# Second scores of a pack-attention soft-MoE kernel in eight small tiles, with wider rows of p, two more weight chunks on chip, plain 32-row output products and products of ones in waits

## The chip, the core and the metric

The kernel runs on one core of a Trainium2 chip. The core has TensorE (PE, matrix products, with its weight loads PEld), VectorE (DVE), ScalarE (ACT), GpSimd (POOL) and SyncE (SP, which here only issues transfers). The metric is the device time of one execution in microseconds (us). All data are float32. A float32 product stands in the trace as two instructions, a transpose as one.

## The reference

Eight batches of eight heads, 576 positions, head dimension 64, 32 packing queries p; then 32 slots on 8 experts.

```python
def sm_attn(qq, kk, vv):
    s = scale * np.matmul(qq, kk.transpose(0, 1, 3, 2))
    s = s - np.max(s, axis=-1, keepdims=True)
    a = np.exp(s)
    a = a / (np.sum(a, axis=-1, keepdims=True) + 1e-09)
    return np.matmul(a, vv)
p_packed = sm_attn(p, k, v)
out = sm_attn(q, p_packed, p_packed)      # second scores: q against p_packed
# x: [4608, 512], phi: [512, 32]
logits = x @ phi
d = softmax(logits, axis=0); slot_input = d.T @ x
for e in range(E):                        # 8 experts, 4 slots each
    slot_out[e] = np.maximum(slot_input[e] @ w1[e], 0.0) @ w2[e]
c = softmax(logits, axis=1)
return c @ slot_out
```

## The kernel before

**Attention in eight steps.** Step i takes two batches and four heads (dd = i // 2 is the pair of batches, g = i % 2 the group of heads). Each step consists of small functions, and the text ORDER lists their calls as name.i.j@bank:engine; each engine works through its own instructions in that order. The functions that the text names: `kt` transposes k on DVE, `s1` are the first scores, `mx1` and `e1` maximum and exponential, `ap`/`apc` transpose the result and copy it, `m` multiplies with v, `ppa`/`pp`/`pt`/`ptc` give the normalized packed values and their transpose ppT, `mp`/`mm` multiply ppT with phi, `qp`/`qc` transpose and copy q, `s2` (L548) are the second scores, `sc` copies them out, `st` (L573) transposes them back, `mx2`, `sb` (L608), `e2` (L631), `z2`, `rc` (L649, L650) and `n2` (L654) make the second softmax, `a2p` (L663) and `a2c` its transpose.

**Logits and slots, once for each pair of batches.** `lg` (L687) adds up the logits of a pair, `f1` to `f6` and `fd` the running softmax over positions, `gr` (L788), `rt`, `gt` (L810), `rb`, `gs` (L847) and `sa` the slot inputs, from which the last call makes xz.

**Experts.** `layer1a` (L934) multiplies xz with w1, `hidden` and `layer1b` transpose and rectify, `layer2` (L986) multiplies with w2 into one bank; `cq`/`cp` (L1004 to L1012) transpose the weights c of the 36 row blocks, split into a high and a low part. The last expert goes to banks of its own in two halves (L1077), is copied (L1095) and summed over its four strips by products with rep (L1098), the sum is split into a high and a low part (L1100, L1101), and 36 output products (L1122, L1129) are copied to the ring and stored.

**Transfers.** SP issues all loads in a fixed list: p of pair 0, k of step 0, the three other p, q and v of step 0, then k, q, v of each step, then w1 and w2 in chunks of 1 MB (32 in all, the last as two halves). They go to a ring of 14 chunks; a load is issued when the space next in the ring is free, which the last reader of a k, q, v or weight piece reports. At the call `late` six further chunks go to `ext`, in the space that the attention's tiles leave. At most eight transfers are under way: each waits for the one eight before it. phi is loaded on ACT's queue at the start.

A second score of step i, for the part j of the row blocks (4, 1 and 4 of the nine), is in before four products over all 128 rows into 64 columns, of which half of the 128 rows are zeros in ppT:

```python
nc.tensor.matmul(
    ps[64 * x : 64 * x + 64, bank, c : c + R * (n1 - n0)].rearrange("p (n r) -> p n r", n=n1 - n0),
    ppTs[i % 2][:, x, b2, o : o + 2].rearrange("p v s -> p (v s)"),
    qT[:, b2, n0:n1, 64 * x : 64 * x + 64], start=True, stop=True)
```

Of the kernel before, what the change touches and what calls it, by code (L numbers as in the profile page):

```python
# [100 lines left out]
def pack_attention_soft_moe(  # L101
# [1067 lines left out]
```

## Time and profile before

| what | value |
|---|---|
| median of three runs | 213.82 us (213.2 to 216.62) |
| the profiled execution, its own time | 215.42 us |
| its span, first to last instruction | 213.6 us |
| mean granted TensorE clock | 0.927 |
| busy: PE, DVE, ACT, POOL | 175.1, 129.8, 102.8, 47.7 us |
| moved by the DMA engines | 72.27 MB, 338 GB/s over the span |

The page cuts the span in 40 slices of 5.34 us; a digit is a busy share in tenths, PEclk the granted TensorE clock in tenths of full speed (9 is 90% or more, 5 the lower of its two levels, 1.2 of 2.4 GHz). A busy PE is not PE at its peak, since matrix products are pipelined and their ends modelled. The attention runs to about 130 us, the last logits and slots to 147.65 us, the experts to 184.85 us, the output from 187.81 us on.

### The profile page before, as it was taken

To read this page: it belongs to the slowest core of one execution; us is meant where nothing else is said; L and a number is where in the kernel's file an instruction comes from. 1 tells how busy PE (TensorE), PEld (TensorE's weight loads), DVE (VectorE), ACT (ScalarE), POOL (GpSimd) and SP (SyncE) were. 2 spreads that over 40 slices of the span, in tenths; PEclk is the share of its full clock that TensorE was granted. 3 is DMA by queue.
4 is the path that set the end of the run, shared out by engine and by line. 5 is a ranking of instruction groups with operands and counts; after the bars stand their busy time and mean duration, and the time that the engine had idled before them with its cause. 6 is when DMAs were issued, how large, how long until landed. Compare 5 with 4: busy or idle time off the path is not lost.

```text
span 213.6 us, 5804 instructions
## 1 busy us (share of the span) xinstructions
PE 175.1 (82%) x2403; PEld 114.8 (54%) x2403; DVE 129.8 (61%) x306; ACT 102.8 (48%) x250; POOL 47.7 (22%) x75
## 2 busy tenths in 40 slices
PE   2399899999799999999999975776999999797000
PEld 1177586877656966768887555343233433374000
DVE  1649578979468786986547698245722475299000
ACT  3035656969539758859656564120211111289000
POOL 7200002754006363063171554003000000000000
PEclk9999999999999999999999997558799999999655
DMA  6999999999999999978429999950699999169997
GB/s 168 283 375 394 391 391 389 388 391 387 394 388 390 391 394 408 347 264 315 183 88 413 361 414 420 426 242 0 218 423 428 422 419 407 47 230 410 410 421 299
DMA packets 24730, 72.27 MB, mean 338 GB/s; under 512 B 4224, under 2 KB 4480, under 8 KB 22784
## 3 DMA queue, kind: packets, MB, share of 16 engines
q1 hardware_dynamic: 24128, 71.83, 87.5%
q8 instruction: 19, 0.31, 0.6%
q10 hardware_dynamic: 576, 0.07, 0.2%
q14 instruction: 7, 0.06, 0.1%
HBM read 62.46 MB, written 9.44 MB: 337 GB/s over the span
## 4 chain that ended last, share of the span: by engine, by line
PE 44%; DMA 25%; DVE 14%; ACT 7%; issue 2%; ACTq 0%; SPq 0%; DVEq 0%
DMA ring<-in_moe_w_dram 13%; PE ps L524 6%; DMA ring<-in_k_dram 6%; PE ps L433 6%; PE ps L663 4%; PE ps L548 3%; PE ps L1129 3%; DMA phi_sb<-in_moe_phi_dram 3%; PE ps L380 3%; DMA ring<-in_v_dram 3%; PE ps L573 3%; PE ps L788 3%; PE ps L934 3%; DVE kT L366 2%; PE ps L411 2%; PE ps L687 2%
## 5 line engine op out<-in xcount | busy, mean ns | idle before, releaser
L366 DVE STREAM_TRANSPOSE kT<-ring 128x576 f32<-128x576 f32 x32 | 23.0, 754 | 6.7 <-DMA ring<-in_k_dram 5.2
L331 ACT COPY qT<-ps 128x512 f32<-128x512 f32 (+1 forms) x45 | 20.6, 492 | 10.9 <-PE ps L524 10.6
L639 POOL TENSOR_TENSOR zt<-a 128x576 f32<-128x576 f32 x7 | 10.0, 1426 | 69.6 <-ACT a L631 51.0
L524 PE MATMUL ps<-ident,ring 128*128 128x128 f32 x144 | 22.9, 292 | 0.7 <-DVE a L608 0.5
L548 PE MATMUL ps<-qT,ppT 128*64 128x256 f32 (+1 forms) x192 | 19.0, 335 | 1.2 <-ACT ppT L331 1.0
L524 PEld LDWEIGHTS ps<-ident,ring 128*128 128x128 f32 x144 | 17.5, 151 | 4.1 <-issue 2.1
L433 PE MATMUL ps<-ring,a1T 64*64 64x128 f32 x576 | 18.3, 273 | 1.6 <-DVE a L608 1.3
L654 POOL TENSOR_TENSOR a<-a,zs 128x1152 f32<-128x1152 f32 (+1 forms) x8 | 16.4, 2050 | 11.2 <-DVE zs L650 7.4
L380 PE MATMUL ps<-kT,pT 32*32 32x288 f32 x512 | 14.9, 446 | 4.2 <-DVE kT L366 4.2
L433 PEld LDWEIGHTS ps<-ring,a1T 64*64 64x64 f32 x576 | 15.6, 133 | 4.1 <-DVE a L608 1.5
L580 DVE TENSOR_REDUCE mx<-ps 128x16 f32<-128x512 f32 (+1 forms) x24 | 12.9, 543 | 3.8 <-PE ps L573 3.4
L548 PEld LDWEIGHTS ps<-qT,ppT 128*64 128x64 f32 x192 | 11.0, 136 | 7.6 <-issue 3.3
L934 PE MATMUL ps<-ring,xz 128*32 128x512 f32 x112 | 14.2, 660 | 0.6 <-DVE xz L1019 0.6
L331 ACT COPY a1T<-ps 128x384 f32<-128x384 f32 x24 | 10.9, 487 | 5.9 <-PE ps L411 5.8
L331 ACT COPY a2T<-ps 128x384 f32<-128x384 f32 x24 | 10.7, 491 | 6.0 <-PE ps L663 5.9
L663 PE MATMUL ps<-ident,a 128*128 128x128 f32 x72 | 11.4, 296 | 2.2 <-DVE a L654 2.2
L391 DVE TENSOR_REDUCE nm<-ps 128x2 f32<-128x1152 f32 x8 | 10.7, 1344 | 3.3 <-PE ps L380 3.3
L331 ACT COPY s2T<-ps 128x512 f32<-128x512 f32 (+1 forms) x19 | 9.2, 491 | 6.3 <-PE ps L548 6.3
L608 DVE TENSOR_TENSOR a<-ps,mx 128x256 f32<-128x256 f32 x32 | 11.9, 418 | 0.4
L380 PEld LDWEIGHTS ps<-kT,pT 32*32 32x32 f32 x512 | 7.0, 107 | 9.3 <-issue 4.8
L394 ACT ACTIVATE a<-ps,nm 128x576 f32<-128x576 f32 x16 | 11.8, 746 | 0.3 <-DVE nm L391 0.3
L573 PE MATMUL ps<-ident,s2T 128*128 128x128 f32 x72 | 11.7, 278 | 0.2
(143 smaller groups left out, 296.4 us busy)
## 6 DMA issues: line engine op xcount, KB each, us to landing
ring<-in_moe_w_dram SPq DMA_DIRECT2D x25, 1024.0 KB, 8.5
ring<-in_k_dram SPq DMA_DIRECT2D x16, 576.0 KB, 11.9
ring<-in_q_dram SPq DMA_DIRECT2D x16, 576.0 KB, 11.9
ring<-in_v_dram SPq DMA_DIRECT2D x16, 576.0 KB, 12.0
out_dram<-ring SPq DMA_DIRECT2D x10, 768.0 KB, 8.5
ext<-in_moe_w_dram SPq DMA_DIRECT2D x6, 1024.0 KB, 13.8
ring<-in_moe_w_dram SPq DMA_DIRECT2D x2, 512.0 KB, 17.9
out_dram<-ring SPq DMA_DIRECT2D x2, 512.0 KB, 4.7
```

The lines of the kernel that those rows point to most:

```text
L331: nc.scalar.copy(dst, src)
L366: nc.vector.transpose(kT[:, b2, :, c].rearrange("p m (t r) -> p m t r", t=T), view(f"k{i}.{b2}").rearrange("p (m t c d) -> p m t c d", m=2 ...
L380: nc.tensor.matmul(ps[32 * y : 32 * y + 32, z, 0 : 32 * T], pT[rs, dd, m, b2, g, c], kT[rs, b2, m, c], start=(c == 0), stop=(c == 1),)
L433: nc.tensor.matmul(ps[64 * b2 : 64 * b2 + 64, b + x, 0:P].rearrange("p (m d) -> p m d", m=2), a1T[rs, t, b2], view(f"v{i}.{b2}").rearrange ...
L524: nc.tensor.transpose(ps[:, bank, o : o + P], view(f"q{i}.{b2}")[:, P * n : P * n + P], ident)
L548: nc.tensor.matmul(ps[64 * x : 64 * x + 64, bank, c : c + R * (n1 - n0)].rearrange("p (n r) -> p n r", n=n1 - n0), ppTs[i % 2][:, x, b2, o ...
L573: nc.tensor.transpose(ps[:, bank, o : o + P], s2T[:, n].rearrange("p b r -> p (b r)"), ident)
L580: nc.vector.tensor_reduce(mxs[i % 2][:, n0:n1].rearrange("p n a -> p (n a)"), ps[:, banks["st", i, j], 0 : P * (n1 - n0)].rearrange("p (a ...
L608: nc.vector.tensor_tensor(a[:, x, j // 2 : T - 1 + j // 2, 1 - j // 2].rearrange("p (n v) s -> p n v s", v=2), src[:, x], m[:, x].unsqueez ...
L654: (nc.vector if eng == "v" else nc.gpsimd).tensor_tensor(a, a, z.unsqueeze(3).broadcast_to([P, a.shape[1], a.shape[2], NS]), op=ALU.mult)
L663: nc.tensor.transpose(ps[:, bank, o : o + P], a2s[i // NG % 2][:, t, i % NG].rearrange("p c s -> p (c s)"), ident,)
L934: nc.tensor.matmul(ps[32 * a : 32 * a + 32, b + nh, :], xzf[:, (4 * e + a) * NSLOT : (4 * e + a + 1) * NSLOT], wv[:, j, nh * 512 : (nh + 1 ...
```

## The change

1. `s2` for the parts 0 and 2 is called per batch b2 instead of per part and gives both: 8 products of 64 rows into 32 columns, in two row groups that write two banks, so 16 in place of 8 a step; the zero half of ppT is no longer multiplied. Part 1 stays at four products over 128 rows. `s1` is called in two halves (by batch), `lg` in two (by step), `gt` makes eight products of half width, `px` works in 32-row groups and once for the pairs 1 to 3.
2. p is loaded as 128 rows of 1024 bytes (before 512 pieces of 256 bytes). phi's four loads move from ACT's queue to SP's, behind v of step 0.
3. `late` gives seven chunks to `ext`; one more chunk (the second of w1 of expert 3) goes to the tile a2_1 at the call `lx`, behind the last `gr`. xz, hidden and the slot sums move into tiles of the attention.
4. `w` calls stand in the waits at the start and in the last logits: products of ones, w.n of 128 n columns, whose results nobody reads.
5. c is transposed as plain float32, four row blocks in one (9 transposes in place of 36), the high and low parts go, the last expert adds to the bank of the others, and each output product takes 32 rows: four of them stand in four row groups.
6. ORDER is written anew. The last `n2` of step 7 is on DVE in both of its parts (before one was on POOL).

```diff
     def f_s2(i, j, bank, eng):
-        for b2 in range(2):
-            for x in range(2):
...
-                    ppTs[i % 2][:, x, b2, o : o + 2].rearrange("p v s -> p (v s)"),
-                    qT[:, b2, n0:n1, 64 * x : 64 * x + 64],
+        b2 = j // 2
+        for x in range(2):
+            for m in range(2):
+                n0, n1 = nk(2 * m)
+                for u in range(2):
+                    us = slice(64 * u, 64 * u + 64)
+                    a = 2 * x + (u + m) % 2
+                    nc.tensor.matmul(
+                        ps[
+                            32 * a : 32 * a + 32,
+                            banks["s2", i, 2 * u],
+                            4 * R * b2 : 4 * R * b2 + 4 * R,
+                        ].rearrange("p (n r) -> p n r", n=4),
+                        ppTs[i % 2][us, x, b2, 2 * (1 - m) + u],
+                        qT[us, b2, n0:n1, 64 * x : 64 * x + 64],
...
     def rows_p(dd):
-        return p[2 * dd : 2 * dd + 2].rearrange("b (g h) s d -> (h s) (b g) d", g=NG)
+        return p[2 * dd : 2 * dd + 2].rearrange("b h (s j) d -> (b h s) (j d)", j=4)
...
+    def f_lx(i, j, bank, eng):
+        key = f"w1_{LX[0]}_{LX[1]}"
+        where[key] = (a2f, 2 * FF)
+        load(a2f[:, 0 : 2 * FF], rows_w1(*LX))
...
-    for x, xs in enumerate(halves):
-        nc.scalar.copy(sh[:, xs], ps[:, 2 + x, xs])
-        nc.vector.tensor_tensor(sh[64:P, xs], ps[64:P, 2 + x, xs], shf[64:P, xs], op=ALU.subtract)
+    for x, (xs, eng) in enumerate(zip(halves, "va")):
+        copy(eng, sh[:, xs], ps[:, 2 + x, xs])
...
-            nc.tensor.matmul(ps[:, b], cT[:, dd * T + order[t]], sh, start=True, stop=True)
+                nc.tensor.matmul(ps[:, b], cT[rs, n4], sh[rs], start=True, stop=True)
```

Two lines of ORDER, the last ones after the change:

```
a2p.7.2@5 rb.2.0 a2c.7.2:a w.1.0@0 gs.2.0 lg.3.1 xz.0.0 sa.2.0
f1.3.0 w.2.0@0 f2.3.0 f3.3.0 w.4.0@0 w.1.0@0 f4.3.0 f5.3.0
```

**Where instructions stand on PE, step 1.** First before, from the packed values of step 1 (L475) on: L548 is s2, with columns and elements of the output behind the names.

```order
L475 MATMUL ps<-ident,pp_157 128x128 x2
L380 MATMUL ps<-kT,pT 32x288 x32
L548 MATMUL ps<-qT,ppT_161 64x256 x8
L548 MATMUL ps<-qT,ppT_161 64x64 x4
L497 MATMUL ps<-phi_sb,ppT_161 64x32 x4
L573 MATMUL ps<-ident,s2T 128x128 x4
```

And in the changed kernel, where L505 is pt, L595 and L578 are s2's two forms and L410 is s1 (of the next steps):

```order
L505 MATMUL ps<-ident,pp_158 128x128 x2
L527 MATMUL ps<-phi_sb,ppT_162 64x32 x4
L595 MATMUL ps<-qT,ppT_162 32x256 x16
L554 MATMUL ps<-ident,ring 128x128 x4
L410 MATMUL ps<-kT,pT 32x288 x16
L622 MATMUL ps<-ident,s2T 128x128 x4
```

Eight products into 64 columns have become sixteen into 32, and part 1 (L578) stands some rows further down, apart from them.

**Where instructions stand on PE, last logits and slots.** Before, from the transposes of the last second softmax (L663) to the first product with w1 (L934):

```order
L663 MATMUL ps<-ident,a_1_109 128x128 x9
L847 MATMUL ps<-rb,pp_156 64x64 x2
L847 MATMUL ps<-rb,pp_157 64x64 x2
L687 MATMUL ps<-a2T_153,mm_162 32x288 x4
L687 MATMUL ps<-a2T_154,mm_163 32x288 x4
L699 MATMUL ps<-ident,nml 1x128
L721 MATMUL ps<-ones,m_185 128x1
L729 MATMUL ps<-dm,ones 128x32
L760 MATMUL ps<-rw,ones 128x32
L788 MATMUL ps<-a_1_109,d 32x256 x18
L810 MATMUL ps<-rep,rt 128x32 x4
```

After it, from the first half of lg (L732) on; L866 are the products of ones:

```order
L732 MATMUL ps<-a2Tb,mm_163 32x288 x4
L866 MATMUL ps<-ones 128x384
L708 MATMUL ps<-ident,a_1_117 128x128 x6
L866 MATMUL ps<-ones 128x128
L708 MATMUL ps<-ident,a_1_117 128x128 x3
L866 MATMUL ps<-ones 128x128
L893 MATMUL ps<-rb,pp_157 64x64 x2
L893 MATMUL ps<-rb,pp_158 64x64 x2
L732 MATMUL ps<-a2Tb,mm_164 32x288 x4
L866 MATMUL ps<-ones 128x256
L744 MATMUL ps<-ident,nml 1x128
L866 MATMUL ps<-ones 128x512
```

The first half of lg has moved ahead of the last transposes, of which only three stand behind the last n2, and products of ones stand between all of these.

**SP's queue at the start**, after the change (L182 is phi, L173 all other loads):

```order
L173 DMA ring<-in_p_dram 128x256
L173 DMA ring<-in_k_dram 128x2x576 x2
L173 DMA ring<-in_p_dram 128x256 x3
L173 DMA ring<-in_q_dram 128x2x576 x2
L173 DMA ring<-in_v_dram 128x2x576 x2
L182 DMA phi_sb<-in_moe_phi_dram 64x2x32 x4
```

phi's four issues are new in this queue, behind v of step 0 and ahead of k of step 1; the p issues stand where they stood.

## Rows read from the trace of the kernel before

**Rows 1.** The page, part 2: granted clock and GB/s in 40 slices of 5.34 us.
```profile
PEclk9999999999999999999999997558799999999655
GB/s 168 283 375 394 391 391 389 388 391 387 394 388 390 391 394 408 347 264 315 183 88 413 361 414 420 426 242 0 218 423 428 422 419 407 47 230 410 410 421 299
```
**Rows 2.** Windows by stage: length, busy us (instructions) by engine, granted clock, DMA share, GB/s.
```profile
28.00:122.00 94.00, 91.23 (x1575) 69.31 (x1575) 70.42 (x171) 66.68 (x168) 34.41 (x38) 1.00 0.93 348
98.00:112.00 14.00, 13.85 (x263) 11.88 (x261) 7.53 (x24) 9.63 (x26) 5.45 (x7) 1.00 0.45 165
132.20:147.65 15.45, 11.12 (x92) 6.67 (x92) 5.78 (x21) 2.98 (x9) 2.07 (x2) 0.58 0.65 268
147.65:184.85 37.20, 36.64 (x328) 13.76 (x328) 18.70 (x44) 5.27 (x8) 0.00 (x0) 0.95 0.83 339
184.85:187.81 2.96, 1.90 (x7) 1.25 (x8) 1.28 (x3) 1.49 (x4) 0.00 (x0) 1.00 0.00 0
187.81:213.60 25.79, 8.50 (x36) 5.92 (x34) 9.49 (x16) 9.89 (x20) 0.00 (x0) 0.73 0.91 367
```
**Rows 3.** Timeline of the issuing queues (SPq, ACTq): start us, us, what.
```profile
1.04 1.38 ACTq L273 DMA_DIRECT2D phi_sb<-in_moe_phi_dram  x2
2.28 4.71 SPq L169 DMA_DIRECT2D ring<-in_p_dram  x3
109.35 0.88 SPq L169 DMA_DIRECT2D ring<-in_moe_w_dram  x2
120.99 8.09 SPq L169 DMA_DIRECT2D ext<-in_moe_w_dram  x6
150.57 16.59 SPq L169 DMA_DIRECT2D ring<-in_moe_w_dram  x13
```
**Rows 4.** DMA queues, ACT's own (phi): packets, MB, share of 16 engines' span.
```profile
q10 hardware_dynamic: 576, 0.07, 0.2%
```
**Rows 5.** The chain that ended last: start us, us, what.
```profile
15.36 12.56 DMA ring<-in_k_dram
...
60.21 0.38 PE ps L548 x8
...
114.52 1.01 PE ps L548 x8
...
117.83 1.25 PE ps L548 x16
```
**Rows 6.** Groups by line on PE: rows*columns of the array, count, busy us, mean ns.
```profile
L433 PE MATMUL ps<-ring,a1T 64*64 64x128 f32 x576 | 18.3, 273 | 1.6 <-DVE a L608 1.3 <-ACT a1T L331 0.3
L548 PE MATMUL ps<-qT,ppT 128*64 128x256 f32 x128 | 16.4, 388 | 1.2 <-ACT ppT L331 1.0 <-DVE a L600 0.2
L380 PE MATMUL ps<-kT,pT 32*32 32x288 f32 x512 | 14.9, 446 | 4.2 <-DVE kT L366 4.2
L1012 PE MATMUL ps<-identr,c 128*128 128x128 f32 x36 | 4.6, 257 | 0.2
```
**Rows 7.** Timeline of the last logits and slots: start us, us, instruction, count.
```profile
120.67 1.18 PE L687 MATMUL ps<-a2T,mm 128*32 128x288 f32 x16
126.60 1.49 PE L788 MATMUL ps<-a,d 64*32 64x256 f32 x36
129.98 1.21 DVE L649 TENSOR_SCALAR zs<-zs 128x12 f32<-128x12 f32 x1
131.49 0.56 DVE L654 TENSOR_TENSOR a<-a,zs 128x384 f32<-128x384 f32 x1
132.19 2.15 PE L663 MATMUL ps<-ident,a 128*128 128x128 f32 x9 [2.16 <-DVE a L654]
134.90 2.15 PE L687 MATMUL ps<-a2T,mm 128*32 128x288 f32 x16
141.70 2.77 PE L788 MATMUL ps<-a,d 64*32 64x256 f32 x36
```
**Rows 8.** Timeline of the end: the subtraction that makes the low part.
```profile
186.51 0.86 DVE L1101 TENSOR_TENSOR sh<-ps,sh 64x256 fp32r<-64x256 f32 x2 [1.20 <-ACT sh L1100]
```

More of the change, by code (lines that the diff above doesn't have):

```diff
@@ L176, in pump @@
             key, width, src = loads[state["next"]]
+            if key == "phi":
+                nc.sync.dma_start(out=width, in_=src)
+                state["next"] += 1
+                continue
             if "at" not in state:
@@ new lines, in layer2 @@
+    def layer2(e, js=range(NJ)):
+        last = e == E - 1
+        for xs in halves if last else (slice(0, DM),):
+            for j in js:
+                a = (j + 2 * (xs.start > 0)) % 4
+                nc.tensor.matmul(
+                    ps[32 * a : 32 * a + 32, SO, xs],
+                    hTf[:, (NJ * e + j) * NSLOT : (NJ * e + j + 1) * NSLOT],
+                    w2v(e, j)[:, xs],
+                    start=(e == 0 and j < 4),
+                    stop=(last and j >= 6),
+                )
+        for j in js:
+            if j % 4 == 3 and not last:
+                release(f"w2_{e}_{j // 4}")
@@ L1019, in pack_attention_soft_moe, with cp @@
+    def cp(n0, n1, eng):
+        bank = 6 + n0 // 4 % 2
+        for n in range(n0, n1):
+            nc.tensor.transpose(
+                ps[:, bank, (n - n0) * P : (n - n0 + 1) * P],
+                Lf[:, 4 * n : 4 * n + 4].rearrange("p t s -> p (t s)"),
+                ident,
+            )
+        copy(
+            eng,
+            cT[:, n0:n1].rearrange("p n x -> p (n x)"),
+            ps[:, bank, 0 : (n1 - n0) * P],
+        )
     nc.vector.tensor_tensor(
@@ L1047, in pack_attention_soft_moe @@
     layer2(1)
+    layer2(2)
     ees.close()
@@ L1102, in pack_attention_soft_moe @@
+    for xs, eng in zip(halves, "va"):
+        copy(eng, so[:, xs], ps[:, SO, xs])
+    for x, xs in enumerate(halves):
+        nc.tensor.matmul(ps[:, 2 + x, xs], repf, so[:, xs], start=True, stop=True)
+    for x, (xs, eng) in enumerate(zip(halves, "va")):
+        copy(eng, sh[:, xs], ps[:, 2 + x, xs])
     for key in ("w2_7_0", "w2_7_2", "w2_7_3"):
         release(key)
-    obank = [4, 5, 6, 7, 0, 1, 2, 3]
-    load = {"a": 0.0, "v": 0.0}
-    order = [4 * (t % 2) + t // 2 for t in range(T - 1)] + [T - 1]
+    obank = [4, 6, 7, 0, 1, 5, 2, 3]
@@ L1109, in pack_attention_soft_moe @@
+    work = {"a": 0.0, "v": 0.0}
     n = 0
```

491 lines of the change are left out of this document (230 added, 261 removed).

## The prediction

> **What bounds the kernel now.** I read the windows by stage first, then the GB/s slices, the queue of SP, the chain, and last the groups by line.
>
> From 28 to 122 us PE is busy for 91.23 of 94 us, DVE for 70.4 and ACT for 66.7 [rows 2]. This stage, steps 2 to 7 of the attention, is PE's. Ahead of it the loads set the pace: the chain holds k of step 2 from 15.36 to 27.92 us [rows 5], and the first two slices of the GB/s row stand at 168 and 283 against some 391 later [rows 1]. Later the loads run ahead until the ring is full: from 98 to 112 us only 165 GB/s flow [rows 2], and SP issues its next batch of w1 at 109.35 [rows 3]. From there 12.6 MB, twelve chunks, flow (the 88 of slice 21 and the six slices behind it), until 141.9 us by the 242 of slice 27; then nothing flows until SP issues again at 150.57 [rows 1, 3], since ring and `ext` are full. Meanwhile the last logits and slots run on PE at a mean granted clock of 0.58 [rows 2]: PE had stood idle for 2.16 us behind the last n2 (the release in front of L663) [rows 7], and the PEclk row falls from 9 to 5 there [rows 1]. The experts are PE's again, 36.64 of 37.20 us [rows 2], with the last chunk just behind. The output is the DMA's: 25.79 us with PE, DVE and ACT under 10 [rows 2].
>
> The sum is made against the profiled execution: span 213.6, own time 215.42, so 1.8 us lie outside the span. The median of the three runs is 1.6 us lower.
>
> **Start: 2.5 us earlier.** At 391 GB/s the first three slices (5.34 us each; 168, 283, 375) lose 3.0, 1.5 and 0.2 us, 4.7 in all [rows 1]. Some 2.2 of these I leave to the first landing, which no edit touches. SP stands 4.71 us on three p issues in small pieces, and q of step 0 behind them [rows 3]; with rows of 1024 bytes that goes. Bounds 0 and 4.7, taken 2.5, since a transfer cannot land at once. The four phi issues are new in SP's queue ahead of k of step 1: 1.38 us for two [rows 3], 2.8 us in all, hidden by six loads of 0.59 MB (9 us of flow) already issued; without these the next k would be 2.8 later. The Trainium skill, "DMA: Bandwidth & Descriptors" (quick facts at its head), wants 512 bytes in a transfer for line rate, and phi's rows of 128 stay below it; by that rule the move into SP's ring would slow the loads behind it. The row says how much: phi's packets took 0.2% of 213.6 us, 0.4 us [rows 4]. With it the start would gain 2.1 instead of 2.5. The products of ones at the start stand where PE waits for p and k, and cost nothing.
>
> **Second scores: 0.8 us a step.** Before, a part of 256 columns is 8 instructions in 1.01 us; part 1, a quarter as wide, is 8 in 0.38 when it stands alone and adds 0.24 (1.25 for 16) when it adjoins [rows 5]. So a group that stands apart pays 0.14, and 0.87 of the 1.01 is columns: 0.85 ns a column and instruction, two instructions at a time. L548's 256-column instructions take 16.4 us in all, 128 ns each [rows 6]. After, the two parts are 32 instructions on eight tiles. No row has that tile. Bounds: if only the four column groups overlapped, 32 of them would take what 16 take now, gain 0; if all eight did at the pace of the nearest rows, L433 (64-row tiles, 18.3 us by 576, 32 ns) and L380 (all 16 tiles, 29 ns) [rows 6], 32 take 0.93 to 1.02 us, with the 0.14 some 1.1 in place of 2.02 for two parts, gain 0.9. L433 is the nearest, as its row groups overlap too. Part 1 now stands apart from them in another tile form and costs 0.38 instead of 0.24, so 0.8 is left. The Trainium skill, "TensorEngine Tiling (Array Packing)", Key Properties, says that changing the tiling mode drains the engine; that is how I read the 0.14, and a rule against splitting the form. Without that loss the gain would be 0.9 a step, 0.6 us more over six steps.
>
> Only steps 2 to 7 count, as the ones before them wait for loads: by 122 us 2.5 + 6 x 0.8 = 7.3, at 109.35 (some 4.5 steps) 6.1. The other edits of the attention (s1 and lg in halves, sb and gt in other pieces) have the same elements and lie in PE's queue as before: nothing.
>
> **Last logits and slots: 5.2 us.** On DVE, L649 takes 1.21 us beside POOL's n2 [rows 7]; with that n2 on DVE (twice the 0.56 of L654) and no such wait, the last n2 ends about 0.5 earlier. From its end (132.05) to the end of lg (137.05) now 5.0 us pass [rows 7]. After: three transposes 0.4 and their copy 0.5, beside them fl, rb and gs, then half of lg, 0.6 at the full-clock row (1.18 for 16) [rows 7]; with gs in front 2.1. Gain 2.9. gr takes 2.77 at half clock and 1.49 at full [rows 7], gain 1.3. The other 4.0 of PE's 11.12 us in this window (less 2.15, 2.15 and 2.77) would shrink by 1.7 at full clock (0.58 to 1) [rows 2, 7]; I take half, 0.8, since DVE and ACT stand between these steps. Against that stand the ones in f3: w.4 and w.1 are 640 columns in two instructions each, 1.09 us at 0.85 ns, in a wait of some 0.7 to 0.8; 0.3 lost. Sum 5.2. What queues behind a product of ones is PE's next real product, and everything behind it. So xz comes at 147.65 - 7.3 - 5.2 = 135.15.
>
> **Experts: to 166.3.** PE's 36.64 us lose 3.6 of the 4.6 of L1012 (9 transposes for 36) [rows 6], and 1.9 of half clock (0.95 over 37.2 us means 3.7 us at the lower level) [rows 2]: 31.1, so PE alone ends at 166.3. The loads: 1 MB at 420 GB/s [rows 1] is 2.5 us. Before, the 12 chunks from 109.35 on were in at 141.9, that is 30 + 2.55. Now the stop at 142 goes: seven chunks in `ext`, one in a2_1, and by the time these are in (135 to 139) xz is there and the ring is being released. So all 24 remaining chunks flow in one go: 109.35 - 6.1 + 2.55 + 60 = 165.8, and half a us for the last products, 166.3. The chunk in a2_1 is issued behind gr (135.15 - 3) and behind the queue, lands about 139.5 to 140.5, and is the eighth that layer1a wants, some 6 us after xz: just in time, and two us more would not move the loads' end.
>
> **End: 0.5 us.** Of 2.96 us from the last product to the first store [rows 2] half of the 0.86 of L1101 and its handoff go [rows 8]: 2.45. The output products in four row groups lie under the stores, 25.8 us against 8.5 of PE [rows 2]; without overlap they would need some 28 and add 2 to 5.
>
> Sum: 166.3 + 2.45 + 25.8 + 1.8 = 196.4. Forecast **196.5 us**, 8% below the median.
>
> **Rivals.** (a) The eight tiles do not overlap, or ACT and DVE (67 and 70 of 94 us) hold steps back, so that the steps gain nothing: loads end at 109.35 - 2.5 + 62.55 + 0.5 = 169.9, xz at 140.0, PE at 171; the end at **201**. L380 and L433 speak against the first, the 24 us of slack on ACT and DVE against the second. (b) The ones do not hold the clock and, at half of it, stand in the way (w.4, 512 columns, then takes 1.7 us): the 5.2 are gone and the 1.9 stay, 140.35 + 33.0 = 173.4 and 30.05 behind: **203.5**. For it: the clock fell while PE was a third idle; against: the ones fill what was idle. (c) Both the start and the steps at their upper bounds (4.7 and 0.9): xz at 132.4, loads end at 163.7, **193.7**. (d) Slower: with a twentieth less work on PE, the attention leaves idle stretches in which the clock falls, as it did at 130 us. It decides from 21.6 us of PE work at the lower level on (196.5 to 218.1, one us lost for each): about **220**. Against it: PEclk is 9 in all 24 slices up to 128 us, the first two with PE mostly waiting among them [rows 1]. (e) No change: the ring stays full just as long, because the order of releases moved, and the new chunks wait for tiles; the 62.55 us of loads would have to start at 121, 18 us later than I put it: **214**; nothing in the rows points there.
>
> **Chances.** Forecast (193 to 200) 0.60, (c) 0.13, (a) 0.12, (b) 0.08, (e) 0.03, (d) 0.04. The range that leaves out no more than 2 in 10 reaches from (c), less the 1.6 us by which the median lies under the profiled run and as much again for the tail, to the edge of (b): 190.5 to 203. Faster by over 2% (about what this measurement can tell from no change) 0.92, within 2% 0.04, slower 0.04.
>
> **What would show it.** Right: GB/s in slice 2 near 390; L595 near 1 us for 32 instructions; PEclk 9 up to the output; no 0 in the GB/s row between attention and experts; xz near 135, the last chunk near 166; the last stretch of stores unchanged at 25.8. Wrong: L595 at 2 us (a); PEclk of 5 between 120 and 140 and L866 at 1.7 us (b); a dip of GB/s at 90 to 110 as long as before (e).

## The result and the profile after

The changed kernel takes 209.3 us (median of four runs, 206.6 to 211.1) beside 215.2 us of the kernel before: ratio 0.970, interval 0.962 to 0.978. Measured once more on another chip (c0, below) it is 207.6 us, ratio 0.965, 0.958 to 0.972. Medians are over all executions; ratios, and the differences drawn below, leave out those that ran in a slower state. So the change gains 3 to 3.5%, not the 8% of the forecast, and the time lies above the range. The profiled execution took 206.58 us, with a span of 204.8.

From the page of the kernel after, granted clock and GB/s in slices of 5.12 us, to be held against [rows 1]:

```profile
PEclk9999999699999999999999999999999999999555
GB/s 211 392 378 392 391 391 389 392 393 386 392 391 392 391 393 407 382 52 342 273 128 414 285 176 416 419 416 422 414 418 422 416 421 364 14 301 410 416 412 305
```

These signs came as forecast: slice 2 at 392 in place of 283, 1.09 us for 32 instructions of L595, no 0 between attention and experts, the clock at 9 through the last logits, a last stretch of 25.4 us. These did not: xz comes at 144 us and the last chunk near 174 (forecast 135 and 166), the ring is full as long as before (52, 342, 273, 128), and the clock has a dip in slice 8 that the kernel before does not have.

Windows by stage of the kernel after, columns as in [rows 2]:

```profile
28.00:122.00 94.00, 88.94 (x1647) 63.11 (x1645) 77.83 (x185) 58.31 (x144) 34.72 (x39) 0.98 0.89 333
144.04:176.05 32.01, 31.88 (x298) 11.50 (x297) 9.26 (x13) 3.19 (x5) 1.40 (x1) 1.00 0.94 386
176.05:179.38 3.33, 2.69 (x28) 1.75 (x28) 0.85 (x2) 1.15 (x4) 0.00 (x0) 1.00 0.00 0
179.38:204.80 25.42, 8.74 (x62) 5.19 (x56) 9.39 (x16) 9.89 (x20) 0.00 (x0) 0.70 0.92 371
```

Experts (37.2 to 32.0 us) and output (25.8 to 25.4) are as forecast. Between 28 and 122 us PE is a little less busy than before (88.9 for 91.2 us), and DVE more (77.8 for 70.4), since copies moved to it from ACT (58.3 for 66.7). The first product with w1 starts at 144.04, though, 3.6 us earlier than before and not 12.5. Where the rest was lost is seen at an event that both kernels have, the last second scores of step 7. From the timelines, before and after (start us, us, instruction):

```profile
121.78 1.08 PE L548 MATMUL ps<-qT,ppT 128*64 128x256 f32 x8
```
```profile
122.49 1.09 PE L595 MATMUL ps<-qT,ppT 64*32 64x256 f32 x32
144.04 3.23 PE L982 MATMUL ps<-ring,a2Tb 128*32 128x512 f32 x28
```

They end at 122.86 before and at 123.58 after: the attention, forecast to be 7.3 us shorter, is 0.7 us longer. From there to the first product with w1 it was 24.8 us and is 20.5. So all the gain up to the experts is behind the second scores, and the question is what became of 8.0 us ahead of them. On PE itself the second scores are nearly as cheap as forecast. The group of the kernel before with its part 1, and the groups of the kernel after (L410 to be held against L380, 14.9, in [rows 6]):

```profile
L548 PE MATMUL ps<-qT,ppT 128*64 128x256 f32 (+1 forms) x192 | 19.0, 335 | 1.2 <-ACT ppT L331 1.0
```
```profile
L410 PE MATMUL ps<-kT,pT 32*32 32x288 f32 x512 | 18.4, 410 | 1.7 <-issue 1.3 <-DVE kT L395 0.3
L595 PE MATMUL ps<-qT,ppT 64*32 64x256 f32 x256 | 10.0, 413 | 0.5 <-ACT ppT L345 0.5
L578 PE MATMUL ps<-qT,ppT 128*64 128x64 f32 x64 | 3.5, 231 | 0.4 <-DVE ppT L349 0.4
```

L595 and L578 make 13.5 us for 19.0, 5.5 less (12.6 and 6.4 less in a11, below, where none of it runs at half clock); L410, the first scores in halves, costs 3.5 more. Two places are new. From the timeline of the kernel after, 31 to 36 us and 112 to 121 us:

```profile
30.85 1.43 POOL L684 TENSOR_TENSOR zt<-a 128x576 f32<-128x576 f32 x1 [24.39 <-ACT a L676]
31.50 0.81 DVE L475 TENSOR_SCALAR rz<-rz 128x2 f32<-128x2 f32 x1
33.85 0.71 PE L410 MATMUL ps<-kT,pT 32*32 32x288 f32 x13 [1.32 <-issue]
35.86 0.43 PE L527 MATMUL ps<-phi_sb,ppT 128*64 128x32 f32 x8 [0.94 <-issue]
...
112.26 2.13 POOL L699 TENSOR_TENSOR a<-a,zs 128x1152 f32<-128x1152 f32 x1 [1.77 <-DVE zs L695]
112.64 1.77 DVE L475 TENSOR_SCALAR rz<-rz 128x2 f32<-128x2 f32 x1
118.15 1.16 ACT L676 ACTIVATE a<-a 128x1152 f32<-128x1152 f32 x1 [3.04 <-DVE a L658]
119.22 0.50 ACT L487 ACTIVATE pt<-ps,rzm 128x64 f32<-128x64 f32 x2
```

At 31 us PE runs dry: first scores of step 2 stop for 1.32 us in front of their last 13 instructions, then nothing is left but to wait for the chain of step 1 (rz L475, pp, pt, ptc, mp L527). At 112 us `rz.7`, an operation on two columns that takes 0.13 to 0.16 us in five of its eight calls, takes 1.77 beside n2.5 on POOL; mx2.6, sb.6, e2.6 (L676) and, behind e2.6 on ACT, ppa.7 (L487) are late by it, and the last second scores wait for ppa.7.

Two windows of the kernel after show the first place:

```profile
30.00:36.00 6.00, 3.75 (x109) 2.32 (x100) 5.21 (x11) 2.02 (x5) 4.13 (x6) 1.00 1.05 390
36.00:40.00 4.00, 4.00 (x68) 2.03 (x74) 3.46 (x9) 3.12 (x7) 1.25 (x1) 0.57 1.06 391
```

PE is busy for 3.75 of 6 us, and then the granted clock is 0.57 for four us.

### The profile page after: what moved, and what is told of

The parts are those of the page before. It is cut to its first block, busy times and chain, and to the rows that moved or that the text cites. A ratio compares the mean times of both kernels' runs of the same rounds, so it can differ in the third digit from the quotient of the medians.

```text
span 204.8 us, 6221 instructions
## 1 busy us (share of the span) xinstructions
PE 176.6 (86%) x2621; PEld 108.9 (53%) x2621; DVE 130.4 (64%) x303; ACT 92.8 (45%) x222; POOL 45.7 (22%) x72
## 4 chain that ended last, share of the span: by engine, by line
PE 44%; DMA 18%; DVE 14%; ACT 7%; issue 4%; POOL 3%; SPq 2%; ACTq 0%; DVEq 0%; POOLq 0%
DMA ring<-in_moe_w_dram 13%; PE ps L410 7%; PE ps L463 7%; PE ps L554 5%; DMA ring<-in_v_dram 5%; PE ps L708 3%; PE ps L595 3%; PE ps L622 3%; DVE a L658 2%; DVE mx L629 2%; ACT ring L345 2%; SPq L173 2%; PE ps L732 2%; PE ps L1154 2%; PE ps L441 2%
## 5 line engine op out<-in xcount | busy, mean ns | idle before, releaser
L684 POOL TENSOR_TENSOR zt<-a 128x576 f32<-128x576 f32 x7 | 10.0, 1424 | 72.6 <-ACT a L676 72.6
L395 DVE STREAM_TRANSPOSE kT<-ring 128x576 f32<-128x576 f32 x32 | 23.2, 753 | 1.6 <-DMA ring<-in_k_dram 1.5
L345 ACT COPY qT<-ps 128x512 f32<-128x512 f32 (+1 forms) x38 | 17.9, 497 | 9.7 <-PE ps L554 9.3
L410 PE MATMUL ps<-kT,pT 32*32 32x288 f32 x512 | 18.4, 410 | 1.7 <-issue 1.3
L463 PE MATMUL ps<-ring,a1T 64*64 64x128 f32 x576 | 18.7, 273 | 1.2 <-DMA ring<-in_v_dram 0.9
L463 PEld LDWEIGHTS ps<-ring,a1T 64*64 64x64 f32 x576 | 15.8, 133 | 3.5 <-DMA ring<-in_v_dram 1.2
L699 POOL TENSOR_TENSOR a<-a,zs 128x1152 f32<-128x1152 f32 x7 | 14.9, 2131 | 7.0 <-DVE zs L695 5.8
L658 DVE TENSOR_TENSOR a<-ps,mx 128x256 f32<-128x256 f32 (+1 forms) x48 | 14.5, 351 | 0.6
L421 DVE TENSOR_REDUCE nm<-ps 128x2 f32<-128x1152 f32 x8 | 10.8, 1346 | 5.8 <-PE ps L410 5.8
L982 PE MATMUL ps<-ring,a2Tb 128*32 128x512 f32 x112 | 14.4, 594 | 0.0
L866 PE MATMUL ps<-ones 128*128 128x512 f32 (+3 forms) x30 | 12.7, 526 | 1.0 <-DVE ones L148 1.0
L345 ACT COPY a1T<-ps 128x384 f32<-128x384 f32 x20 | 9.3, 488 | 8.5 <-PE ps L441 8.5
L410 PEld LDWEIGHTS ps<-kT,pT 32*32 32x32 f32 x512 | 8.4, 105 | 8.3 <-issue 4.3
L441 PE MATMUL ps<-ident,a 128*128 128x128 f32 x72 | 11.0, 280 | 0.8 <-ACT a L424 0.8
L708 PE MATMUL ps<-ident,a 128*128 128x128 f32 x72 | 10.5, 281 | 1.2 <-DVE a L699 0.7
L687 POOL TENSOR_TENSOR zt<-zt 128x288 f32<-128x288 f32 (+2 forms) x21 | 11.1, 530 | 1.6
L345 ACT COPY a2Tb<-ps 128x384 f32<-128x384 f32 (+1 forms) x16 | 7.3, 468 | 9.2 <-PE ps L708 4.3
```

What stands on the lines that cost most here:

```text
L345: nc.scalar.copy(dst, src)
L395: nc.vector.transpose(kT[:, b2, :, c].rearrange("p m (t r) -> p m t r", t=T), view(f"k{i}.{b2}").rearrange("p (m t c d) -> p m t c d", m=2 ...
L410: nc.tensor.matmul(ps[32 * y : 32 * y + 32, z, 0 : 32 * T], pT[rs, dd, b2, g, c, m], kT[rs, b2, m, c], start=(c == 0), stop=(c == 1),)
L441: nc.tensor.transpose(ps[:, bank, o : o + P], a1[:, t].rearrange("p x r -> p (x r)"), ident)
L463: nc.tensor.matmul(ps[64 * b2 : 64 * b2 + 64, b + x, 0:P].rearrange("p (m d) -> p m d", m=2), a1T[rs, t, b2], view(f"v{i}.{b2}").rearrange ...
L658: nc.vector.tensor_tensor(dst, a, b.unsqueeze(len(w) - 1).broadcast_to(w), op=ALU.subtract)
```

## Experiments

In each group the kernels ran on one chip beside the kernel before; medians in us, ratios with their interval. Names like a8 shorten the labels.

### The change taken back piece by piece

**c0**, the changed kernel again.

> The changed kernel once more, as the measure for the runs beside it. All theories: the ratio to the kernel before that was found first, 0.970 within 0.008, a span near 204.8 us. If the pause of PE at 32.5 to 36 us and the granted clock of 0.55 to 0.60 at 36 to 40 us belong to the order of the work, they stand in this execution too, within 0.5 us of the same places; if they were an accident of one execution, PE goes on there, the clock stays at 1.00, and the span is 1.5 to 3 us shorter.

As above: 207.6 us, span 205.6. The pause of 13 instructions stands at 34.70 (1.45 us) and the dip of the clock in the same slice. The pause belongs to the order: it is in every profile below that leaves this stretch as it is. The dip does not. a6 and a10, whose edits lie behind the attention, and a7 leave PE idle there for about as long and keep the clock; it falls behind 122 us instead. Windows and page of a10:

```profile
30.00:36.00 6.00, 3.61 (x102) 2.18 (x94) 5.22 (x11) 1.73 (x5) 4.42 (x6) 1.00 1.06 390
36.00:40.00 4.00, 4.00 (x84) 2.61 (x81) 3.58 (x9) 3.12 (x8) 0.96 (x1) 1.00 1.06 391
PEclk9999999999999999999999975799999999999655
```

Nor does the dip cost anything at the last second scores. Executions reach the attention at different times: the products m of step 1 (L463) begin at 27.6 us (a9) to 29.5 us (c0) in profiles whose kernels are the same up to there. Counted from there, the last call of part 1 (L578) starts after 93.3 and 93.5 us with the dip (the kernel after, c0) and after 93.7 to 93.9 without it (a10, a6, a7). Without it PE stops once more, at 50 us (0.83 us in a10).

**a1**, first scores in one call. In step 5 kt.6.0 overwrites a part of k ahead of this call, so those products work on other data of the same size.

```diff
-        b2 = j
+        if j == 0:
+            return
         for c in range(2):
-            for y in range(2 * b2, 2 * b2 + 2):
+            for y in range(4):
```

> The changed kernel with the first scores in one call again (all 16 tiles, 64 instructions at the place of the second half). Theory (the halves cost 3.5 us of PE, since each has only two of the four column groups): L410 falls from 18.4 to about 14.9 us, xz and the end come 2 to 3.5 us earlier, ratio 0.954 to 0.961. Rival (these 3.5 us lie in waits for the second softmax on POOL and for loads): L410 falls as much, but the time stays within 0.7 us. Second rival (the first half started work early that now waits for the last kt): up to 2 us slower.

206.1, 0.961 (0.952 to 0.969): about 1 us less. The group falls even to 14.0 us, but PE idles more:

```profile
PE ps L411 <- issue: 1.6, 1, 1.6
PE ps L506 <- DVE pp L493: 1.3, 2, 1.0
PE ps L411 <- DVE kT L395: 0.9, 1, 0.9
```

(waits of PE in a1, total, times, longest). Nearer to the rival.

**a2**, second scores and sb as before, called at the new places.

```diff
-        b2 = j // 2
-        for x in range(2):
-            for m in range(2):
...
+        n0, n1 = nk(j)
+        o = (2, 1, 0)[j]
+        for b2 in range(2):
+            for x in range(2):
...
+                    ppTs[i % 2][:, x, b2, o : o + 2].rearrange("p v s -> p (v s)"),
+                    qT[:, b2, n0:n1, 64 * x : 64 * x + 64],
```

> The changed kernel with the second scores as before: eight products of 128 rows into 64 columns for the parts 0 and 2, half of them zeros, at the same two places; sb as before. Theory (PE sets the pace of the attention): L595 and L578 go from 13.5 to some 19.5 us, of which six steps count: 4 to 5 us slower, ratio 0.990 to 0.995. Rival (the wait chain over POOL and the loads set the pace): the time grows by less than 1.5 us, PE's idle time takes the rest.

210.3, 0.982 (0.976 to 0.988): 3.1 us more than c0 by the medians, 3.7 by the ratios. L583, which holds all its second scores, is 18.6 us. Between the two expectations.

**a3**, no products of ones (w) in the last logits.

```diff
-z2.7.1:v a2c.6.0:a w.4.0@0 lg.3.0@7 rc.7.1 n2.7.1:v z2.7.2:v w.3.0@0
+z2.7.1:v a2c.6.0:a lg.3.0@7 rc.7.1 n2.7.1:v z2.7.2:v
...
-f1.3.0 w.2.0@0 f2.3.0 f3.3.0 w.4.0@0 w.1.0@0 f4.3.0 f5.3.0
+f1.3.0 f2.3.0 f3.3.0 f4.3.0 f5.3.0
```

> The changed kernel without the eleven products of ones in the last logits and slots (those at the start stay). Theory (they hold the clock): granted clock 0.5 to 0.6 between 129 and 145 us, gr at 2.7 instead of 1.4 us, xz some 3 us later, half clock into the experts, the end 2 to 4 us later, ratio 0.98 to 0.99. Rival (the ones stand in the way of real products and the loads set the end of the experts anyway): the time within 0.7 us of the changed kernel, or shorter.

209.8, 0.977 (0.972 to 0.983): 2.4 us more. gr of a3, then windows, first to its product with w1, then behind it:

```profile
139.34 2.77 PE L833 MATMUL ps<-a,d 64*32 64x256 f32 x36
130.00:145.47 15.47, 9.46 (x92) 5.38 (x92) 8.19 (x26) 2.88 (x9) 1.41 (x2) 0.62 1.01 418
145.47:160.00 14.53, 14.53 (x116) 4.64 (x120) 6.98 (x8) 1.75 (x2) 1.40 (x1) 0.81 0.82 326
```

The clock falls to 0.62, as before the change (0.58), and stays low into the experts (0.81). xz comes only 0.5 to 1.4 us later than in c0 and the kernel after, but this execution started earlier: from the end of the last second scores to xz it takes 22.8 us in place of 20.5, and from xz to the end 61.9 in place of 60.7. So two thirds of the loss lie ahead of xz, half of that in gr (2.77 us in place of 1.49).

**a4**, p in 512 pieces of 256 bytes.

```diff
-        return p[2*dd : 2*dd+2].rearrange("b h (s j) d -> (b h s) (j d)", j=4)
+        return p[2*dd : 2*dd+2].rearrange("b (g h) s d -> (h s) (b g) d", g=NG)
```

> The changed kernel with p loaded in 512 pieces of 256 bytes again, as before; the pieces land at other places of the same tile, so the products work on p in another arrangement. Prediction's step (the start is worth 2.5 us, and all that comes behind moves with it): 2.5 us slower than the changed kernel. Theory (the lead of the start is lost between 30 and 40 us, where PE waits for the chain of step 1 and its clock falls): the first k lands some 2 to 3 us later, but the end is under 1.2 us later.

208.3, 0.971 (0.964 to 0.978), on another chip than c0: 0.6 to 1.3 us more. The first kt comes at 6.27 in place of 4.86 (4.80 to 5.73 in the profiles with wide rows), so 1.5 us at most was there to gain.

**a6**, six chunks in ext, none in a2_1.

```diff
-NEXT = 7
+NEXT = 6
-    LX = (3, 1)
+    LX = None
-fd.3.0 w.4.0@0 f6.3.0 gr.3.0@4 lx.0.0 gz.3.0
+fd.3.0 w.4.0@0 f6.3.0 gr.3.0@4 gz.3.0
```

> The changed kernel with six chunks in ext and none in a2_1, as before. If the loads set the end of the experts (the chain of the changed kernel ends in 27 us of loads): two chunks of 2.5 us move behind xz, 4 to 5 us slower. If PE sets it (33.4 of 34 us busy there): under 1 us slower, and the last chunk lands later without moving the end.

211.7, 0.987 (0.981 to 0.994): some 4 us more. Loads and PE end the experts together, and two chunks behind xz are felt nearly in full.

**a7**, no products of ones at the start.

```diff
-p.0.0 w.4.0@0 w.1.0@0 px.0.0@4 kt.0.1 pc.0.0:a kt.0.0 w.4.0@0 w.2.0@0 s1.0.0@0
+p.0.0 px.0.0@4 kt.0.1 pc.0.0:a kt.0.0 s1.0.0@0
```

> The changed kernel without the four products of ones at the start (8 matrix instructions and their 8 weight loads fewer on PE). If they only fill waits: time within 0.7 us, clock 1.00 up to 30 us as in the kernel before, whose PE stood idle there. For the pause at 32.5 us: if PE stops there for its instructions, which are fetched in blocks, the place moves with their number, from 13 instructions in front of the end of s1.2 to some 5; if it stops for data, it stays at 13.

208.3, 0.973 (0.967 to 0.980). They only fill waits. The pause has moved, as the theory of instructions wants (timeline of a7):

```profile
34.85 0.68 PE L410 MATMUL ps<-kT,pT 32*32 32x288 f32 x5 [1.60 <-issue]
```

Eight matrix instructions fewer on PE, and five instead of 13 stand behind the pause.

### The stalls

**a5**, the second softmax of step 0 later, away from rz.1.

```diff
-kt.2.2 e2.0.0 m.1.1 kt.2.1 m.1.2 kt.2.3 z2.0.0:p rz.1.0
+kt.2.2 m.1.1 kt.2.1 m.1.2 kt.2.3 rz.1.0
-rc.0.0 n2.0.0:p pt.1.0 mx1.2.0 ptc.1.1:a ptc.1.0:a
+pt.1.0 mx1.2.0 ptc.1.1:a ptc.1.0:a e2.0.0 z2.0.0:p
-rz.2.0 kt.3.2
+rz.2.0 kt.3.2 rc.0.0 n2.0.0:p
```

> The changed kernel with the second softmax of step 0 moved back: e2.0 and z2.0 behind the copies ptc of step 1, rc.0 and n2.0 behind kt.3.2, so that POOL does not work beside rz.1. Theory (DVE waits beside POOL, rz.1 takes 1.6 us in place of 0.5, and PE, which has nothing else there, loses 2.3 us and then its clock): L475 takes 0.15 us, PE waits 1.0 to 1.3 us less between 31 and 36 us, the clock falls less, the end comes 1 to 3 us earlier. Rival (PE stops there for something else, such as its own instructions, since it stops between the two instructions of one product): the pause of 1.3 us in front of the last 13 instructions of s1.2 stays, and the time is within 0.7 us.

210.2, 0.981 (0.974 to 0.987): slower. L475 takes 0.13 us, yet the pause of 13 instructions is still there (1.73 us): that pause is not DVE's. And n2.0, later by its own delay, is waited for by a2p.0 (2.5 us, "L708 <- POOL a L699"). The theory fell in this form.

**a8**, rz.7 ahead of rc.5.

```diff
-qp.7.5@1 sc.6.0:a rc.5.0 st.6.2@3 qc.7.3:a qc.7.5:v ap.7.1@5 n2.5.0:p ap.7.0@7 rz.7.0
+qp.7.5@1 sc.6.0:a rz.7.0 rc.5.0 st.6.2@3 qc.7.3:a qc.7.5:v ap.7.1@5 n2.5.0:p ap.7.0@7
```

> The changed kernel with rz.7 on DVE one place earlier, ahead of rc.5, so that it does not stand beside n2.5 on POOL. Theory (rz.7 takes 1.77 us there in place of 0.15 in every profile of the changed kernel, and mx2.6, sb.6, e2.6 and ppa.7 come that much later, on the chain to the last second scores): L475 at 0.16 us, e2.6 1.3 to 1.6 us earlier, the last second scores (L595) and xz 1 to 1.6 us earlier, ratio 0.957 to 0.961. Rival (PE is busy there with other work and sets the pace): e2.6 earlier, xz and the end within 0.5 us.

206.2, 0.964 (0.960 to 0.968). Timeline of a8:

```profile
111.79 0.17 DVE L475 TENSOR_SCALAR rz<-rz 128x2 f32<-128x2 f32 x1
116.72 1.17 ACT L676 ACTIVATE a<-a 128x1152 f32<-128x1152 f32 x1 [1.47 <-DVE a L658]
```

e2.6, the last second scores (122.16) and xz (142.61) are all 1.4 us earlier (1.6 counted from the products m of step 1). The theory holds for the chain; the end gains less, 1.0 us by the medians and 0.2 by the ratios, and the ratio is above the expected range.

**a9**, step 1 in another order.

```diff
-kt.2.2 e2.0.0 m.1.1 kt.2.1 m.1.2 kt.2.3 z2.0.0:p rz.1.0 s1.2.0@0 ppa.1.0 ppa.1.1 s1.2.1 pp.1.0 pp.1.1
+rz.1.0 kt.2.2 e2.0.0 m.1.1 kt.2.1 m.1.2 kt.2.3 z2.0.0:p s1.2.0@0 ppa.1.0 ppa.1.1 pp.1.0 pp.1.1 pt.1.0
+ptc.1.1:a ptc.1.0:a s1.2.1
```

> The changed kernel with rz.1 ahead of the last three kt of step 2, and pp.1, pt.1 and ptc.1 ahead of the second half of s1.2 instead of behind it: the chain rz, pp, pt, ptc, mp of step 1 then lies beside s1.2. Theory (here the lead of the start is lost): mp.1 comes 1 to 1.5 us earlier, PE is busy for 8.7 instead of 7.7 us between 30 and 40 us, the clock falls less or not at all, xz and the end come 1 to 3 us earlier. Rival (loads and later waits set the pace; what is saved at 35 us is waited for later): mp.1 earlier, the end within 0.7 us.

206.0, 0.965 (0.958 to 0.972). Windows of a9:

```profile
36.00:40.00 4.00, 3.88 (x59) 2.90 (x61) 3.67 (x9) 2.97 (x7) 0.05 (x1) 1.00 1.05 389
...
116.00:118.00 2.00, 1.09 (x12) 0.43 (x10) 1.22 (x4) 2.00 (x6) 1.12 (x1) 1.00 0.23 18
118.00:120.00 2.00, 1.36 (x19) 0.74 (x11) 1.34 (x4) 0.54 (x3) 1.76 (x4) 0.86 0.96 369
120.00:122.00 2.00, 2.00 (x38) 0.72 (x34) 0.91 (x4) 0.27 (x1) 1.15 (x3) 0.50 1.01 414
```

The dip at 36 us is gone, which it also is in executions without the edit (a10). mp.1 starts at 33.30 in place of 35.86, and e2.6 at 115.58 in place of 118.15, 2.6 us earlier; 1.2 of these this execution had before the edit acts (m of step 1 at 27.60 in place of 28.80), so the edit is worth 1.4. The end gains 1.2 us by the medians and next to nothing by the ratios. In this execution the stall of rz.7, left in, takes it away: PE is busy for 1.09 and 1.36 of 2 us, the clock falls to 0.50 and stays there to 128 us, and xz comes at 145.82. The changed kernel has the same stall; its profiled execution kept the clock there (1.00), those of a6, a7 and a10 did not (0.50 from 124 us). From the end of the last second scores to xz it is 20.5 us where the clock is kept (the kernel after, c0, a8) and 22.7 to 23.7 where it falls (a7; a6, a9, a10). This is probably why the changed kernel's executions lie up to 4.5 us apart.

**a10**, both halves of the first output product ahead of the three other row groups.

```diff
-                    for xs in halves:
-                        for y in range(4):
+                    first((0,))
                     for xs, eng in zip(halves, "av"):
                         copy(eng, ob[:, 0, xs], ps[:, b, xs])
                         nc.sync.dma_start(out=ov[:, 0, xs], in_=ob[:, 0, xs])
+                    first((1, 2, 3))
```

> The changed kernel with the two halves of the first output product ahead of the other three row groups. Theory (the first copy waits for all 16 instructions of L1143, 1.15 us, since the four row groups are called side by side): first store 0.5 to 0.8 us earlier, the end as much. Rival (the first copy waits for its own product alone, and the stores set the end): within 0.2 us in the first store.

210.0, 0.976 (0.966 to 0.987). The first copy starts 1.16 us after L1143, as without the edit: the rival's side. The other row groups cost nothing there; that the four instructions of the first product stand one behind the other in their row group would explain the 1.16 us, but was not tried.

**a11**, a8, a9 and a10 together, and e2.6 with z2.6 behind ppa.7.

```diff
-a2p.5.1@7 e2.6.0 a2p.5.2@5 a2c.5.1:v a2p.5.0@4 ppa.7.0 qp.7.2@3 a2c.5.2:v z2.6.0:p ppa.7.1
+a2p.5.1@7 a2p.5.2@5 a2c.5.1:v a2p.5.0@4 ppa.7.0 qp.7.2@3 a2c.5.2:v ppa.7.1 e2.6.0 z2.6.0:p
```

> The three edits (rz.7, step 1, first output product) together, and e2.6 and z2.6 behind the two ppa.7 on ACT. Theory (the lead is lost at these places, one after the other): last second scores at 119.5 to 121.5 us instead of 123.6, xz at 140 to 142, the end 3 to 5 us earlier, ratio 0.943 to 0.953. Rival (PE and loads take up what is saved): under 1.5 us.

204.7, 0.957 (0.953 to 0.961), all six executions within 0.6 us; measured again (e0) 204.5, 0.949 (0.943 to 0.954). Page of a11:

```profile
PEclk9999999999999999999999999999999999999855
```

No dip; the last second scores end at 120.90, xz comes at 141.44. 2.5 to 3 us against the changed kernel by the medians (1.7 and 3.5 by the ratios of a11 and e0), less than the theory's 3 to 5. Counted from the products m of step 1, the last second scores come 2.8 us earlier, about what a8 (1.6) and a9 (1.4) make together.

### The terms again, without the stalls

Each starts from a11. **d1**: first scores in one call (steps 1, 2, 5, 6, 7 at the first place, else at the second). **d2**: a4's edit. **d3**: a2's.

```diff
-        b2 = j
+        if j == (i in (1, 2, 5, 6, 7)):
+            return
         for c in range(2):
-            for y in range(2 * b2, 2 * b2 + 2):
+            for y in range(4):
```

> The kernel a11_all (with its four edits) with the first scores in one call, at the place of the first half where all four kt stand ahead of it (steps 1, 2, 5, 6, 7), else at that of the second. Theory (with the stalls gone PE sets the pace of the attention, so the 3.5 us that the halves cost are time): L410 at 14 to 15 us, xz and the end 2 to 3.5 us earlier than a11_all, ratio 0.941 to 0.948. Rival (the halves start work that PE would else wait for, as the run of s1 in one call showed at first): within 1 us of a11_all.

> The kernel a11_all with p loaded in 512 pieces of 256 bytes; the pieces land at other places of the same tile, so the products work on p in another arrangement. Theory (the start is worth 2.5 us as predicted, once the wait at 31 to 36 us does not swallow it): 2 to 2.5 us slower than a11_all. Rival (the start is worth no more than in the changed kernel, since PE has slack in the first two steps anyway): 0.7 to 1.3 us slower.

> The kernel a11_all with the second scores as before (eight products of 128 rows). Theory (0.8 us a step over six steps, as predicted, once the stalls are gone): 4 to 5 us slower than a11_all. Rival (part of it lies in waits for DVE and POOL in any case): 2.5 to 3.5 us slower, as in the changed kernel.

d1 204.1, 0.956 (0.949 to 0.962), 0.5 us less than a11. d2 205.9, 0.963 (0.958 to 0.969), 1.2 more. d3 208.6, 0.975 (0.969 to 0.981), 4.0 more. The second scores are worth what the theory said, the start only what a4 showed, the halves hardly anything. Windows of d1:

```profile
28.00:40.00 12.00, 9.85 (x193) 6.72 (x185) 9.26 (x23) 6.38 (x14) 5.38 (x6) 0.86 1.06 388
40.00:60.00 20.00, 18.82 (x400) 13.83 (x400) 17.47 (x40) 12.72 (x34) 5.39 (x6) 1.00 1.05 390
```

PE's saving appears as idle time (18.82 of 20, where a11 has 19.76), and the clock dips again. d1 is no clean reversal: with s1.2 in one call ahead of pt.1, mp.1 comes 7.2 us behind m of step 1 again, as in the changed kernel (7.1; a11 6.0).

**e1**, one call in the steps 5 to 7 alone, where d1 opened few waits, beside e0, a11 again.

```diff
-        b2 = j
+        if i > 4 and j == (i > 5):
+            return
+        ys = range(4) if i > 4 else range(2 * j, 2 * j + 2)
-pt.4.0 kt.6.0 s1.5.1
+pt.4.0 s1.5.1 kt.6.0
```

> The kernel a11_all once more, as the measure for the run beside it: ratio 0.957 within 0.004, all executions within 1 us of each other, granted clock 1.00 from the start to the output.

> The kernel a11_all with the first scores in one call in steps 5 to 7 alone (step 5 at the place of the second half, steps 6 and 7 at that of the first; kt.6.0 behind s1.5). Theory (the halves cost PE time, 0.5 us a step, and only where PE would else wait, in the steps up to 4, do they give it back): L410 falls by 1.3 to 1.6 us, PE has no new waits, xz and the end 1 to 1.6 us earlier than a11_all, no step of the clock below 1.00. Rival (what PE saves in the last steps is waited for too, on DVE and ACT): within 0.5 us of a11_all.

204.2, 0.946 (0.940 to 0.951) beside e0's 204.5 and 0.949: the same. The groups with the most time show why (e1):

```profile
L412 PE MATMUL ps<-kT,pT 32*32 32x288 f32 x512 | 17.0, 409 | 2.0 <-DVE kT L395 1.4 <-issue 0.5
```

1.9 us less on PE, 1.4 of it in waits for kt on DVE. The rival holds: the halves start what can be started while the other half's kt is not there.

**e2**, 20 copies (qc, apc, a2c of steps 1 to 7) back from DVE to ACT, in a11.

```diff
-qc.1.1:v
+qc.1.1:a
-a2c.4.1:v
+a2c.4.1:a
...
```

> The kernel a11_all with 20 copies of the attention (qc, apc and a2c of steps 1 to 7) on ACT, where all but a few of them stood before the change, instead of DVE. Between 28 and 122 us DVE was busy for 70.4 us before and 77.8 after, ACT for 66.7 and 58.3. Theory (DVE, with the copies that the new order gave to it, holds back the rest of the attention's gain): DVE falls to some 68 us, the last second scores and xz 1 to 3 us earlier than in a11_all, ratio 0.938 to 0.948. Rival (PE's and ACT's own chains hold it back): within 0.7 us, or slower by up to 2 us, where a copy now queues behind an exponential.

206.2, 0.954 (0.950 to 0.958): 1.7 us slower than e0. Window of e2:

```profile
28.00:122.00 94.00, 88.81 (x1659) 62.73 (x1665) 67.42 (x167) 63.97 (x161) 34.93 (x39) 1.00 0.91 339
```

DVE falls from 77.6 to 67.4 us as expected, and it does not help: PE now waits for copies on ACT (1.6 us for a2Tb). So the rest does not come from moving DVE's load to ACT; with ACT as free as in a11 it was not tried.

## Why the prediction was wrong, by its steps

**What bounds the kernel** failed in one point. PE, busy for 91 of 94 us, was taken as the pace of the attention, so that its microseconds are time. They are that for the second scores in good part (6.4 us on PE at full clock, 4.0 in time, d3), not for the first (some 4 us on PE, 0.3 to 1 in time; a1, d1, e1). A busy share near 1 held work that starts early because nothing better stood in the queue.

**Start, 2.5 us**: mis-sized. The pieces of p cost at most 1.5 us at the first kt and 0.6 to 1.4 in the end (a4, d2; 1.2 taken). The stall at 31 us did not swallow it: without the stall it is no larger. The upper bound came from GB/s of slices in which the first landing also lies. phi's move, put at nothing, was not tried by itself; slices 2 and 3 (392 and 378 GB/s) show no loss behind it.

**Second scores, 0.8 us a step**: the price on PE was right (1.02 to 1.09 us for 32 instructions on eight tiles), and the sum of 4.8 us is 4.0 where nothing stalls, 3.1 to 3.7 in the changed order.

**"The other edits of the attention ... nothing"**: the step that failed. I asked of each edit whether it had more elements, and of the new ORDER only what stands on PE in two places. It has two stalls that the old one has not: rz.7 beside POOL (1.4 to 1.6 us, a8) and step 1's late chain (1.4 us, a9). Mended together they are worth 2.7 us at the last second scores and 2.5 to 3 at the end (a11). Rival (d), idle stretches in the attention in which the clock falls, came true in part: the half clock at 36 us cost nothing at the last second scores, and where it falls behind 122 us instead, xz comes 2.2 to 3.2 us later. The halves of s1, which I also put at nothing, cost 3.5 us on PE and next to nothing in time: right for a reason not given.

**Sum at the last second scores**: forecast 7.3 us earlier, found 0.7 later. Start explains 1.3 of the 8.0, the size of the second scores 0.8, the stalls 2.7. The other 3.2 stay open: a11 stands 2.0 us ahead of the kernel before, where 1.2 and 4.0 would make 5.2. From 28 us to that event PE is busy for 92.1 of 94.9 us before and for 89.6 of 92.9 in a11, so that little of it is waiting: the first scores take 14.5 us there in place of 9.6, about as much more as the second scores were to give. Yet taking that off PE does not bring it back as time (d1, e1), nor does moving copies from DVE to ACT (e2). The single profiles are also up to 1.9 us apart before that, at m of step 1.

**Last logits, 5.2 us**: 4.3 from the last second scores on. From the last n2 (133.32) to the end of lg (135.25) it is 1.9 us (forecast 2.1, before 5.0), gr takes 1.49 in place of 2.77, and the ones hold the clock (1.00; 0.62 without them). What is missing lies ahead of e2.7: 4.8 us from the last second scores to e2.7 where it was 3.25. Both parts of the second scores are now complete only with the last call, and sc, st, mx2 and sb of both follow in one burst; that reading was not tried by itself. The price of the clock, 1.8 us ahead of xz (1.3, 0.8, less 0.3) and 1.9 behind it, was about right: a3 loses 2.4 and 1.2 us in its profile, and 2.4 in the medians.

**Experts**: 32.0 us behind xz, forecast 31.1, and the two extra chunks are worth some 4 us (a6). The loads failed with the attention: they stop in slices 18 to 21 as long as before, once more in slices 23 and 24 (285, 176), run in one go only from 122.9 us on and end near 174 us, forecast 165.8. A dip as long as before was my sign for rival (e); it came, but its 214 us did not. **End**: 3.33 us in place of 2.45. I took off half of the low part (0.86) and its handoff and left out what the plain float32 product costs: from the first product, four instructions in two halves, to the first copy it is 1.16 us, before 0.42. **Output**: 25.4, forecast 25.8.

## What to carry to other kernels

Price a new order by what each small operation stands beside, on all engines, and not only by the work that it moves: here one operation on two columns, put beside POOL, took back 1.4 of the 4 us that 128 products gave. Microseconds taken from the busiest engine are time only where its next instruction is ready; find one event that both kernels have, and compare its time before dividing a gain among stages. Where an idle stretch may cost the clock, removing it steadies the time as well: a11's executions lie within 0.6 us, the changed kernel's within 4.5.

## What the runs showed of the hardware

- A DVE operation on two columns waited for POOL's running instruction to end. L475 (0.16 us alone) ends at 32.31 and 114.41, POOL's L684 and L699 at 32.28 and 114.39. Transposes from the ring and reductions out of PSUM beside POOL keep their time (L395 0.76 us, L421 1.29 beside L699 at 35 us). The Trainium skill, "SBUF — State Buffer" (SBUF: two separate sides), tells of a port pair that DVE and GpSimd lock for a whole instruction; the trace agrees.
- PE stopped for 1.3 to 1.7 us between the two instructions of one product, in every profile with the changed order of step 1 but a2's, whose PE has fewer instructions ahead, and the place moved with the number of instructions ahead of it (13 to 5 when eight matrix instructions and their weight loads went, a7), not with the data (a5). Ahead of it stand 72 instructions of m and 51 of the first scores without a gap. The traces show what it waits for, PE's own instructions: the page of the kernel after (line below) has a queue of 20 instruction packets of 16 KB, by their number PE's, one for every 262 of its 5242 matrix instructions and weight loads. One lies at 31.43 to 32.55 us; PE stops at 32.53 and goes on at 33.85, 1.3 us behind its end. In all the profiles with the pause PE goes on 1.2 to 1.5 us behind the end of such a packet, and so it does at the stop at 50 us in a10 (packet 47.53 to 48.61 us, PE again at 49.92). The Trainium skill, "Runtime: NRT & Kernel Launch" (Instruction fetch mechanics), has instructions fetched in blocks of 256 and the crossing of a block mostly hidden; here it was not. With pt between the halves of s1 (a9, a11, e0, e1, e2, d2, d3) the pause is 0.5 us or less.

```profile
q8 instruction: 20, 0.33, 0.7%
```

- The granted clock fell to its lower level (1.2 of 2.4 GHz) in the attention too: in the changed kernel after PE had been busy for 3.75 of 6 us (0.57 in the next four), in a9 after 1.09 of 2 us (0.86, then 0.50 up to 128 us, though PE was busy throughout). With PE at 1.12 of 2 us from 118 to 120 us the changed kernel's profiled execution kept it: such a place costs the clock in some executions and not in others, and so does the one at 36 us (0.57 in the kernel after, 1.00 in a10).
- Half a call of 16 tiles is not half its time: 32 of the first scores' instructions on eight tiles take 1.20 us, 64 on sixteen 1.60.
